# Small matmuls of an attention and routing kernel put on column tiles of TensorE, logits of four batches in one go, counts of a group moved to GpSimd

## The chip, the cores and the metric

The kernel runs on one core of one Trainium2 chip. The metric is the device time of one execution in microseconds (us); lower is better. Three runs of the kernel before gave 476.44, 477.48 and 478.11 us, a median of 477.48.

## The reference, cut to what matters

Two blocks follow each other. The first is a linear attention with a state (four batches, eight heads, 768 steps, head size 48); its output, as 3072 rows of 384, goes through a router with eight experts, of which each row takes one.

```python
# per step t; state is [B, H, 48, 48]
cur = einsum('bhd,bhe->bhde', u * kt, vt)
y[:, :, t] = einsum('bhd,bhde->bhe', rt, state + cur)
state = w * state + einsum('bhd,bhe->bhde', kt, vt)
...
# router: rows x [3072, 384], 8 experts
logits = normed(x) @ normed(expert_emb).T / tau
expert_idx = argmax(logits, axis=1)
gate_w = softmax(logits)[row, expert_idx]
out[mask] = gate_w[mask, None] * (relu(x[mask] @ w1[e]) @ w2[e])    # mask: the rows of expert e
```

Everything is float32 (f32).

## The kernel before, in words

The steps are cut into six chunks of 128. A *unit* is one chunk of one batch, 24 in all, unit i being batch i % 4 of chunk i // 4. The four units of one chunk are a *group*; routing is done by group. `attention` (L713) writes out the order of the work by hand: one loop over i from -1 to 30, in each of whose turns a list of small functions adds instructions for this unit, the next, or one that lies behind. `on` calls a function for one unit, `of_group` for one batch of a group, `whole` once in four turns, when the unit it is given is its group's last. Each engine runs its instructions in the order in which the loop wrote them, and a semaphore makes an engine wait for another.

What a turn i does, in TensorE's order:

- `turn` (L298) transposes the R and the scaled K of unit i+1: `rt` (L304), then `kt` (L309), four matmuls each. VectorE multiplies `rt` by powers of the decay (L306), ScalarE copies `kt` (L311).
- `states` (L330) makes the chunk's K'V for unit i, two heads at a time: four matmuls `st` (L339) with 112 columns of weights and 96 columns streamed, of which the diagonal blocks are used. `carry` (L343) adds them to the state on VectorE (L352), and GpSimd multiplies the state by the decay (L356). The last chunk has no `st`.
- `sums` (L359) makes y of unit i: with the state (L369), and with the masked scores, head by head, on two column halves of the array (L372). ScalarE copies it (L378, L382).
- `scores` (L315) makes the scores of unit i+1, `at` (L322), eight matmuls on two row halves; VectorE masks both tiles (L326).
- `rows` (L387) transposes y into rows, `yrows` (L394); VectorE adds the own term and writes X (L398). `own_sum` follows on VectorE (L286); ScalarE scales by it (`own_rows`, L294, eight instructions).
- `turn_rows` (L471) transposes X of unit i-1, `xp` (L476), and ScalarE copies it to xT (L478).
- `logits` (L486) makes the logits of unit i-2: three matmuls `lg` (L491) with xT as weights (128 columns) and eight streamed columns, the experts.
- In some turns: `ranks` (L510), five matmuls that count, for each row of the group, the rows before it with the same expert (L514 to L517), and `taken` (L578), four matmuls that put the group's row numbers into lists (L581).

The routing of a group on the other engines: `choose` (L494) finds each row's expert on VectorE and leaves a one-hot tile `oh`; `gates` (L520) takes a power on GpSimd (L522), an exponential on ScalarE (L526) and steps on VectorE (L523 to L530); `places` (L533) multiplies rank and one-hot (L536, L538) and adds the group's counts to `cum` on GpSimd, four instructions (L540). `listed` (L574) compares and multiplies (L555 to L570), `summed` (L586) adds the list on VectorE.

PSUM is handed out by tag (`Banks`, L1033): two buffers for "tp", which `rt`, `kt` and `yrows` share in turn, two for "at", and one for each of "st" (`st`, `rank`, `take`, `cp`), "y", "xp" and "lg". A tile waits until the readers of the one that had its buffer before are done.

After turn 24 the loop mixes the routing of the last groups with the first tile of two experts (`Early`, L804): `hidden` (L828, two halves of 12 matmuls), `rows` (L840, two halves of four) and `out` (L849). Then comes the expert stage (`expert`, L903), which fills the rest of the run. `load` (L249) asks for K, R and V of unit i + AHEAD at the start of turn i, on SyncE's queue, where `put` (L543) also writes X out.

Of the kernel before, what the change touches and what calls it, by code (L numbers as in the profile page):

```python
# [19 lines left out]
C = 128  # L20
# [6 lines left out]
TM = 4  # L27
# [12 lines left out]
AHEAD = 5  # L40
# [71 lines left out]
def build_consts(k):  # L112
# [37 lines left out]
    k.qt = numbers(k, "qt", [QS, QS], [[TM, 2], [0, E], [1, TM]], 0, 0)  # L150
    k.turned = numbers(k, "turned", [QS, QS], [[0, 2], [1, E], [0, TM]], 1, 0)
    k.part = pool.tile([QS, 1], I32, name="part")
# [9 lines left out]
    k.sums = pool.tile([QS, 128], F32, name="sums")  # L162
# [5 lines left out]
def build_turned(k):  # L168
# [4 lines left out]
    bits = pool.tile([QS, 3], I32, name="bits")  # L173
    nc.vector.tensor_scalar(bits[:, 0:1], k.part, 2, E - 1, ALU.arith_shift_right, ALU.bitwise_and)
    nc.vector.tensor_scalar(bits[:, 1:2], k.part, 3, None, ALU.bitwise_and)
    nc.vector.tensor_scalar(bits[:, 2:3], k.part, 5, 2, ALU.arith_shift_right, ALU.arith_shift_left)
    own = pool.tile([QS, 3], F32, name="own")
    nc.vector.tensor_copy(own, bits)
    nc.vector.tensor_add(own[:, 1:2], own[:, 1:2], own[:, 2:3])
    k.mask = pool.tile([QS, E], F32, name="mask")  # L180
    nc.vector.tensor_scalar(k.mask, k.number[0:QS], own[:, 0:1], None, ALU.is_equal)
# [26 lines left out]
def build_experts(k):  # L208
# [16 lines left out]
    k.ent = k.const.tile([128, NK, E], F32, name="ent")  # L225
    nc.vector.tensor_copy(k.ent, ps)
# [103 lines left out]
def states(k, i):  # L330

    nc = k.nc
    c, b = divmod(i, B)
    if c == NCH - 1:
        return
    V, Kw = k.loaded[i][2], k.Kpad[i % len(k.Kpad)]
    st = k.ps.tile([128, NP, 2 * D], F32, name="st", tag="st")
    for p in range(NP):
        nc.tensor.matmul(st[0:PP, p, :], pair(Kw, p)[:, 0:PP], pair(V, p), start=True, stop=True)  # L339
    k.st[i] = st  # L340


def carry(k, i):  # L343
# [5 lines left out]
    for s in range(2):  # L349
        rows = slice(s * DP, s * DP + D)  # L350
        part = T[rows, :, s * DP : s * DP + D]
        nc.vector.tensor_add(part, part, st[rows, :, s * D : (s + 1) * D])  # L352
# [118 lines left out]
def turn_rows(k, g, b):  # L471
# [5 lines left out]
    g.xT[b] = k.work.tile([128, NK, C], F32, name="xT", tag="xT")  # L477
# [8 lines left out]
def logits(k, g, b):  # L486
    xT = g.xT.pop(b)
    if b == 0:
        g.lg = k.ps.tile([128, B, E], F32, name="lg", tag="lg")
    for m in range(NK):  # L490
        k.nc.tensor.matmul(g.lg[:, b, :], xT[:, m, :], k.ent[:, m, :], start=(m == 0), stop=(m == NK - 1))  # L491
# [17 lines left out]

def ranks(k, g):  # L510

    mm = k.nc.tensor.matmul
    g.rank = k.ps.tile([128, B, E], F32, name="rank", tag="st")
    mm(g.rank, k.umask, g.oh, start=True, stop=False)  # L514
    for b in range(1, B):
        mm(g.rank[:, b:B, :], k.ones, g.oh[:, 0 : B - b, :], start=False, stop=False, skip_group_check=True)
    mm(g.rank, k.ones, k.cum[:, None, :].to_broadcast([128, B, E]), start=False, stop=True)  # L517
# [15 lines left out]
def places(k, g):  # L533
# [5 lines left out]
    for b in range(B):  # L539
        nc.gpsimd.tensor_add(k.cum, k.cum, g.oh[:, b, :])  # L540
# [37 lines left out]
def taken(k, g):  # L578
    g.take = k.ps.tile([QS, 128], F32, name="take", tag="st")
    for b in range(B):  # L580
        k.nc.tensor.matmul(  # L581
            g.take, g.what[:, b].rearrange("p q s -> p (q s)"), g.lane[:, b, :], start=(b == 0), stop=(b == B - 1)
        )
# [73 lines left out]
def turner(k, by):  # L657

    nc, p = k.nc, k.rt
    hit = p.tile([QS, E], F32, name="hit", tag="hit")  # L660
    rank = p.tile([QS, 1], F32, name="myrank", tag="myrank")
    nc.vector.scalar_tensor_tensor(hit, by[0:QS], 1.0, k.mask, ALU.mult, ALU.mult, accum_out=rank)
    perm = p.tile([QS, QS], F32, name="perm", tag="perm")
# [39 lines left out]
def route(k, g):  # L703
    for b in range(B):
# [3 lines left out]
        logits(k, g, b)  # L708
    for step in (choose, ranks, gates, places):
# [3 lines left out]
def attention(k):  # L713
# [17 lines left out]
    for i in range(-1, units + 7):  # L731
# [6 lines left out]
        whole(places, i - 4)  # L738
        on(own_rows, i)
        on(turn, i + 1)  # L740
        on(scaled, i + 2)
# [3 lines left out]
        whole(choose, i - 3)  # L745
        whole(listed, i - 5)
# [11 lines left out]
        of_group(logits, i - 2)  # L758
# [376 lines left out]
```

## Time and profile before

| | |
|---|---|
| runs before, us | 476.44, 477.48, 478.11 (median 477.48) |
| profiled execution, us | 475.24 |
| its span, first to last instruction, us | 473.4 |
| granted TensorE clock over the span | 0.99 |
| busy: TensorE, its weight loads | 447.4 us (95%), 317.5 us (67%) |
| busy: VectorE, ScalarE, GpSimd | 148.8 us (31%), 138.2 us (29%), 171.7 us (36%) |
| moved by DMA | 54.26 MB, mean 115 GB/s |
| 40 to 150 us | the attention's units, one after another |
| 178 to 205 us | routing of the last groups and the two early tiles |
| 205 us to the end | the experts |

All lines of the profile are of one profiled execution of 475.24 us, of which 473.4 lie between its first and last instruction. PE is TensorE's matmuls, PEld its weight loads, DVE is VectorE, ACT is ScalarE, POOL is GpSimd, SP is SyncE, which issues DMAs; L322 is line 322 of the kernel. In a timeline the first number is the start in us from the span's start, the second how long the instruction or the row of like instructions took; x8 is their number, and a bracket tells how long the engine was idle before it and what ended that. Each f32 matmul of the program is recorded as two MATMULs, with a weight load each (transposes as one). The ends of matmuls are modelled and overlap, so the distance between starts is the better measure of what one costs.

### The profile page before, as it was taken

What the parts mean: (1) busy time and instruction counts of PE and PEld (TensorE: products, weight loads), DVE (VectorE), ACT (ScalarE), POOL (GpSimd) and SP (SyncE); (2) the same over time, 40 slices, a digit from 0 to 9 for tenths busy, and PEclk for the clock granted to TensorE, in tenths of its full rate; (3) what the DMA queues carried; (4) which work ended last, traced back from release to release, by engine and by line L of the source; (5) the groups of instructions that cost most, each with busy time, mean ns of one, the idle gap of its engine ahead of it and who ended that gap; (6) DMA issues with size and microseconds to landing.
All of it is one profiled execution on the core that took longest, in us unless ns stands there. A gap on an engine that the chain in (4) does not pass through costs nothing.

```text
span 473.4 us, 7292 instructions
## 1 busy us (share of the span) xinstructions
PE 447.4 (95%) x2716; PEld 317.5 (67%) x2716; DVE 148.8 (31%) x416; ACT 138.2 (29%) x410; POOL 171.7 (36%) x260
## 2 busy tenths in 40 slices
PE   8789999999999889999999999999998999999990
PEld 3578889898989778866765555555555555556550
DVE  4556776566657754230102003003002002011010
ACT  2376655665565561101101201201210200201200
POOL 7766677665856433360204003303301201011010
PEclk9999999999999999999999999999999999999996
DMA  8766645654561393143535125134232243100000
GB/s 177 141 135 136 134 95 108 135 127 106 105 135 35 106 406 123 47 138 133 184 150 200 27 106 198 57 133 149 103 133 87 113 151 120 46 18 32 1 37 19
DMA packets 93791, 54.26 MB, mean 115 GB/s; under 512 B 76937, under 2 KB 88380, under 8 KB 93746
## 3 DMA queue, kind: packets, MB, share of 16 engines
q1 hardware_dynamic: 89024, 43.85, 33.6%
q0 software_dynamic: 3296, 9.44, 5.6%
q10 hardware_dynamic: 1426, 0.41, 0.4%
q8 instruction: 23, 0.38, 0.3%
q14 instruction: 22, 0.18, 0.1%
HBM read 44.45 MB, written 9.63 MB: 114 GB/s over the span
## 4 chain that ended last, share of the span: by engine, by line
PE 79%; DVE 9%; ACT 4%; SPq 2%; issue 2%; DMA 2%; POOL 1%; POOLq 0%; ACTq 0%; DVEq 0%
PE ps L920 26%; PE ps L938 14%; PE ps L928 11%; PE at L322 5%; PE y L372 3%; PE y L369 3%; PE st L339 3%; PE early_h L834 2%; DVE AT L326 2%; ACT xd L294 2%; PE lg L491 2%; PE early_y L845 2%; PE yrows L394 2%; DVE y L940 1%; PE kt L309 1%
## 5 line engine op out<-in xcount | busy, mean ns | idle before, releaser
L920 PE MATMUL ps<-xTe,w 128*128 128x384 f32 (+3 forms) x384 | 120.9, 475 | 3.0 <-DVE xTe L915 2.8
L920 PEld LDWEIGHTS ps<-xTe,w 128*128 128x128 f32 x384 | 72.3, 190 | 48.3 <-issue 22.3
L941 POOL DMA_INDIRECT out_dram<-y,to x25 | 24.7, 987 | 205.0 <-DVE y L940 186.7
L940 DVE TENSOR_SCALAR y<-ps,gates 128x384 f32<-128x384 f32 (+2 forms) x25 | 14.6, 613 | 229.4 <-PE ps L938 125.2
L921 ACT ACTIVATE hT<-ps 128x384 f32<-128x384 f32 (+3 forms) x64 | 30.2, 478 | 165.3 <-PE ps L920 165.2
L938 PE MATMUL ps<-w,hT 128*128 128x384 f32 x208 | 67.9, 486 | 0.0
L938 PEld LDWEIGHTS ps<-w,hT 128*128 128x128 f32 x208 | 39.5, 190 | 27.1
L928 PE MATMUL ps<-hT,w 128*128 128x416 f32 (+1 forms) x144 | 52.0, 521 | 0.0
L294 ACT ACTIVATE xd<-V,diag 128x48 f32<-128x48 f32 x192 | 45.8, 321 | 19.3 <-DVE diag L286 14.9
L928 PEld LDWEIGHTS ps<-hT,w 128*128 128x128 f32 x144 | 27.4, 190 | 24.2 <-issue 24.2
L326 DVE TENSOR_TENSOR AT<-at,umask 128x512 f32<-128x512 f32 x48 | 30.9, 686 | 34.2 <-PE at L322 34.2
L322 PE MATMUL at<-RT,KT 48*128 48x128 f32 x384 | 27.9, 285 | 4.4 <-ACT KT L311 3.4
L356 POOL TENSOR_TENSOR state<-state,wpow 48x192 f32<-48x192 f32 x40 | 20.4, 511 | 28.0 <-DVE state L352 26.5
L887 POOL DMA_INDIRECT G<-xs,take x25 | 25.2, 1008 | 12.2 <-issue 5.8
L322 PEld LDWEIGHTS at<-RT,KT 48*128 48x128 f32 x384 | 23.3, 187 | 9.3 <-ACT KT L311 5.1
L372 PE MATMUL y<-AT,V 128*48 128x128 f32 x384 | 25.9, 277 | 0.0
L280 POOL TENSOR_TENSOR KU<-KU,Rpad 128x384 f32<-128x384 f32 x24 | 24.1, 1003 | 1.9
L271 POOL TENSOR_TENSOR Kpad<-K,kpow 128x384 f32<-128x384 f32 x23 | 23.1, 1003 | 3.3 <-DVE kpow L100 2.0
L279 POOL TENSOR_TENSOR KU<-K,u_bc 128x384 f32<-128x384 f32 x24 | 24.1, 1003 | 0.3 <-DVE diag L286 0.3
L372 PEld LDWEIGHTS y<-AT,V 128*48 128x48 f32 x384 | 19.8, 122 | 3.0
L369 PE MATMUL y<-RT,state 128*112 128x128 f32 x160 | 21.2, 275 | 0.0
L478 ACT COPY xT<-xp 128x384 f32<-128x384 f32 x24 | 11.5, 480 | 31.3 <-PE xp L476 31.3
(183 smaller groups left out, 515.1 us busy)
## 6 DMA issues: line engine op xcount, KB each, us to landing
w<-in_moe_w_dram SPq DMA_DIRECT2D x16, 1536.0 KB, 6.3
K<-in_k_dram SPq DMA_DIRECT2D x24, 192.0 KB, 3.6
V<-in_v_dram SPq DMA_DIRECT2D x24, 192.0 KB, 3.5
xs<-X SPq DMA_DIRECT2D x24, 192.0 KB, 2.0
Rpad<-in_r_dram SPq DMA_DIRECT2D x23, 192.0 KB, 3.6
G<-xs,take POOLq DMA_INDIRECT x27
out_dram<-y,to POOLq DMA_INDIRECT x25
Rpad<-in_r_dram ACTq DMA_DIRECT2D x1, 192.0 KB, 4.0
```

The lines of the kernel that those rows point to most:

```text
L279: nc.gpsimd.tensor_mul(KU, K, k.u_bc)
L294: k.nc.scalar.mul(xd[:, h, :], V[:, h, :], diag[:, h : h + 1])
L322: nc.tensor.matmul(at[s][:, p, :], KT[rows, p, :], RT[rows, p, :], start=True, stop=True)
L326: nc.vector.tensor_mul(a, at[s], k.umask[:, None, :].to_broadcast([128, NP, C]))
L369: mm(y[0:PP, p, :], T[:, p, 0:PP], RT[:, p, :], start=(p == 0), stop=False, skip_group_check=True)
L372: mm(y[s * DP : s * DP + D, p, :], V[:, 2 * p + s, :], AT[s][:, p, :], start=(c == 0 and p == 0), stop=True, skip_group_check=True,)
L887: nc.gpsimd.indirect_dma_start(out=G[0:n, :], out_offset=None, in_=k.xs[:, :], in_offset=IndirectOffsetOnAxis(ap=take[0:n], axis=0), bound ...
L920: mm(ps[:, 0:n], w1[:, m, f * 128 : (f + 1) * 128], xT[:, m, 0:n], start=(m == 0), stop=(m == NK - 1))
L921: nc.scalar.activation(hT[:, f, 0:n], ps[:, 0:n], ACT.Relu)
L928: mm(ps[:, 0:n], w2[:, f, m * 128 : (m + 1) * 128], hT[:, f, 0:n], start=(f == 0), stop=(f == NF - 1))
L938: mm(ps, hT[:, f, at], w2[:, f, :], start=(f == 0), stop=(f == NF - 1))
L941: nc.gpsimd.indirect_dma_start(out=k.out[:, :], out_offset=IndirectOffsetOnAxis(ap=to[0:here], axis=0), in_=y[0:here, :], in_offset=None, ...
```

## The change

Five things, of which four lie on TensorE.

- `states`: one matmul for each head in place of one for two heads, 48 columns of weights and 48 streamed; even heads write rows 0 to 47, odd heads rows 64 to 111, so the two lie on different column halves. `carry` reads the smaller tile.
- `logits`: runs once for a group, with the expert embeddings as weights (32 columns, of which eight are used) and xT streamed (128 columns); batch b goes to column quarter b, four batches side by side. The result has experts on partitions; `logits_out` copies it to SBUF on ScalarE, and `turn_logits` transposes it on TensorE. The tile `lgT` uses the tag "st". xT gets five buffers.
- `ranks`: GpSimd makes the counts ahead of each batch (`before`, one copy and four additions, the last of which updates `cum`), and two matmuls replace five. The additions in `places` go.
- `taken`: batches 0 and 2 sum on one column half, 1 and 3 on the other; the tiles of the lists (`sums`, `qt`, `turned`, `mask`, `hit`, `perm`) have 128 rows in place of 64.
- AHEAD is 4 in place of 5, which gives back the memory of one unit's K, R and V.

```diff
-AHEAD = 5
+AHEAD = 4
...
-    k.ent = k.const.tile([128, NK, E], F32, name="ent")
-    nc.vector.tensor_copy(k.ent, ps)
+    k.ent = k.const.tile([128, NK, 32], F32, name="ent")
+    nc.vector.memset(k.ent, 0.0)
+    nc.vector.tensor_copy(k.ent[:, :, 0:E], ps)
...
 def states(k, i):
-    st = k.ps.tile([128, NP, 2 * D], F32, name="st", tag="st")
+    st = k.ps.tile([128, NP, D], F32, name="st", tag="st")
     for p in range(NP):
-        nc.tensor.matmul(st[0:PP, p, :], pair(Kw, p)[:, 0:PP], pair(V, p), start=True, stop=True)
+        for s in range(2):
+            h = 2 * p + s
+            nc.tensor.matmul(
+                st[s * DP : s * DP + D, p, :], Kw[:, h, 0:D], V[:, h, :], start=True, stop=True, skip_group_check=True
+            )
...
-        nc.vector.tensor_add(part, part, st[rows, :, s * D : (s + 1) * D])
+        nc.vector.tensor_add(part, part, st[rows])
...
-def logits(k, g, b):
-    xT = g.xT.pop(b)
-    if b == 0:
-        g.lg = k.ps.tile([128, B, E], F32, name="lg", tag="lg")
+def logits(k, g):
+    mm = k.nc.tensor.matmul
+    lgT = k.ps.tile([128, 128], F32, name="lgT", tag="st")
     for m in range(NK):
-        k.nc.tensor.matmul(g.lg[:, b, :], xT[:, m, :], k.ent[:, m, :], start=(m == 0), stop=(m == NK - 1))
+        for b in range(B):
+            mm(
+                lgT[b * 32 : (b + 1) * 32, :], k.ent[:, m, :], g.xT[b][:, m, :],
+                start=(m == 0), stop=(m == NK - 1), tile_position=(0, b * 32), skip_group_check=True,
+            )
+    g.lgT = lgT
+def logits_out(k, g):
+    t = k.rt.tile([128, 128], F32, name="lgT", tag="lgT")
+    k.nc.scalar.copy(t, g.lgT)
+    g.lgT = t
+def turn_logits(k, g):
+    lg = k.ps.tile([128, B, 32], F32, name="lg", tag="lg")
+    k.nc.tensor.transpose(lg.rearrange("q b e -> q (b e)"), g.lgT, k.ident)
+    g.lg = lg[:, :, 0:E]
...
+def before(k, g):
+    nc = k.nc
+    g.pre = k.rt.tile([128, B, E], F32, name="pre", tag="pre")
+    nc.gpsimd.tensor_copy(g.pre[:, 0, :], k.cum)
+    for b in range(1, B):
+        nc.gpsimd.tensor_add(g.pre[:, b, :], g.pre[:, b - 1, :], g.oh[:, b - 1, :])
+    nc.gpsimd.tensor_add(k.cum, g.pre[:, B - 1, :], g.oh[:, B - 1, :])
 def ranks(k, g):
     mm(g.rank, k.umask, g.oh, start=True, stop=False)
-    for b in range(1, B):
-        mm(g.rank[:, b:B, :], k.ones, g.oh[:, 0 : B - b, :], start=False, stop=False, skip_group_check=True)
-    mm(g.rank, k.ones, k.cum[:, None, :].to_broadcast([128, B, E]), start=False, stop=True)
+    mm(g.rank, k.ones, g.pre, start=False, stop=True)
...
 def places(k, g):
-    for b in range(B):
-        nc.gpsimd.tensor_add(k.cum, k.cum, g.oh[:, b, :])
...
 def taken(k, g):
-    g.take = k.ps.tile([QS, 128], F32, name="take", tag="st")
+    g.take = k.ps.tile([2 * QS, 128], F32, name="take", tag="st")
     for b in range(B):
         k.nc.tensor.matmul(
-            g.take, g.what[:, b].rearrange("p q s -> p (q s)"), g.lane[:, b, :], start=(b == 0), stop=(b == B - 1)
+            g.take[b % 2 * QS : (b % 2 + 1) * QS], g.what[:, b].rearrange("p q s -> p (q s)"), g.lane[:, b, :],
+            start=(b < 2), stop=(b >= B - 2), skip_group_check=True,
         )
...
 def attention(k):
         whole(places, i - 4)
+        whole(logits_out, i - 3)
         on(own_rows, i)
         on(turn, i + 1)
+        whole(turn_logits, i - 3)
         on(scaled, i + 2)
         on(own, i + 1)
         on(states, i)
         of_group(squares, i - 1)
         whole(choose, i - 3)
+        whole(before, i - 3)
         whole(listed, i - 5)
...
         of_group(turn_rows, i - 1)
-        of_group(logits, i - 2)
+        whole(logits, i - 2)
         whole(ranks, i - 3)
         whole(gates, i - 3)
```

## The prediction

> **What bounds the kernel now.** First the page's slices: from 40 us on TensorE is at 9 to 10 tenths in nearly every slice, and the chain that ended last is TensorE's.
>
> ```profile
> PE   8789999999999889999999999999998999999990
> PE 79%; DVE 9%; ACT 4%; SPq 2%; issue 2%; DMA 2%; POOL 1%; POOLq 0%; ACTq 0%; DVEq 0%
> ```
>
> Busy isn't bound, so next the timeline of one plain unit of the attention:
>
> ```profile
> 94.18 0.60 PE L394 MATMUL yrows<-ident,yT 112*128 112x112 f32 x4
> 94.28 1.29 DVE L326 TENSOR_TENSOR AT<-at,umask 128x512 f32<-128x512 f32 x2 [1.36 <-PE at L322]
> 94.62 0.49 PE L476 MATMUL xp<-ident,X 128*128 128x128 f32 x3
> 94.95 0.73 PE L491 MATMUL lg<-ent,xT 128*128 128x8 f32 x6
> 95.49 0.55 DVE L398 TENSOR_TENSOR X<-yrows,xd 128x384 f32<-128x384 f32 x1
> 95.54 0.64 PE L304 MATMUL rt<-ident,Rpad 128*128 128x128 f32 x4
> 96.18 0.63 PE L309 MATMUL kt<-ident,Kpad 128*128 128x128 f32 x4
> ```
>
> The "tp" buffers hand yrows' place to kt, so kt waits for X, and X waits behind the two maskings on DVE. X ends at 96.04; kt starts 0.14 later. In the other plain units it is the same. So kt starts 2.0 us after yrows whatever TensorE does between; it has 0.1 to 0.2 to spare there already. Counting from yrows to yrows, a group takes 6.32 (plain), 7.24 (with take), 6.32 (its choose) and 7.80 (with ranks): 27.68 us, four times over. In the last of these another DVE chain ends late:
>
> ```profile
> 145.39 0.16 DVE L536 TENSOR_TENSOR at<-rank,oh 128x32 f32<-128x32 f32 x1
> 145.60 0.53 PE L339 MATMUL st<-V,Kpad 128*112 128x96 f32 x3 [0.32 <-DVE at L536]
> ```
>
> st waits for places to read rank (they share a bank), and places stands behind X, diag and the gates, not behind TensorE's ranks. Last the tail, where TensorE is full and each routing step hides beside an early tile:
>
> ```profile
> 182.71 2.92 PE L834 MATMUL early_h<-earlyx,w 128*128 128x128 f32 x24
> 182.90 0.19 DVE L498 TENSOR_REDUCE mx<-lg 128x4 f32<-128x32 f32 x1 [0.49 <-PE lg L491]
> 183.79 0.19 DVE L504 TENSOR_TENSOR oh<-oh,first 128x32 f32<-128x32 f32 x1
> 185.47 0.31 PE L514 MATMUL rank<-oh,umask 128*128 128x32 f32 x2
> 185.67 0.60 ACT L838 ACTIVATE earlyh<-early_h 128x512 f32<-128x512 f32 x1 [3.96 <-PE early_h L834]
> 186.51 2.83 PE L845 MATMUL early_y<-w,earlyh 128*128 128x384 f32 x8
> 188.98 0.40 POOL L570 TENSOR_TENSOR what<-sel,gate 128x128 f32<-128x128 f32 x1
> 189.44 1.09 PE L581 MATMUL take<-lane,what 128*64 128x128 f32 x8
> ```
>
> The choice of experts (182.9 to 184.0) lies wholly under early_h.
>
> [...] y's matmuls on two halves (L372) start in pairs 7 ns apart, a pair every 109 ns, and wherever the mode changes 203 ns pass in place of 109: a drain of 94. The first weight load is then exposed too. [...] with few columns streamed, 128 of weights give 111 ns a MATMUL (L491), 112 give 98 (L339), and L372's loads of 48 follow 42 apart. [...]
>
> **Part by part.** The sum is made against the profiled 475.24 us (span 473.4); the median 477.48 lies 2.24 above, and the difference is carried over.
>
> *st, 20 units, 16 of them (4 to 19) in the steady stage; in the first four, ACT's chain (diag, eight xd, KT) sets the pace.* Before: 8 x 98 = 785 ns. After: 16 MATMULs in 8 pairs. A pair costs the larger of 48 streamed columns (48/128 of 109 = 41) and the load (42), say 45: 360. The mode changes add 94+42 going in and 94+93 (y's 112 columns) coming out: 683. Gain 0.10. After ranks the drain hides in the wait, and the exposed load shrinks from 76 to 42: 861 to 589, gain 0.27. No row streams pairs this fast: L372 sustains 27 ns per MATMUL or load, and at that pace a pair is 109 and st 1195, a loss of 0.41; bounds -0.1 to +0.41. I take 45, since at 84.27 to 84.32, where L372 begins, four loads and two MATMULs start within 48 ns.
>
> *logits.* Removed from plain units: 6 x 111 = 0.67 each, worth nothing, since kt waits for X. In one turn of four: 24 MATMULs, four at a time, 6 x 109 = 654, entry 94+28, exit 94+59: 0.93. xp and yrows 0.77, rt 0.44, so kt at 2.14 instead of 2.0: +0.14, and the transpose +0.11. Two at a time (the only packing in the trace) would make it 0.65 more; less than 6 rounds can't be. logits_out queues on ACT ahead of xd, but ends (about 2.05) before diag frees xd (2.4), and before kt ends, so the transpose finds it ready.
>
> *ranks.* 10 MATMULs of 112 become 4, 0.67 less, worth nothing: X and then places set the end. `before` (five ops of about 0.23 to 0.26) moves past the state's multiply and the power on POOL: the power ends at 142.4, DVE asks at 143.97; one op more fits. *take.* 8 x 109 to 4 x 109: kt would be free at 1.94, so X binds and the unit falls from 7.24 to 6.32: -0.92. Bounds 0 (no pairing) to -0.92.
>
> *AHEAD, ent, the 128-row lists.* Nothing: K lands 3.6 us after its issue and is asked for units later. Load 5 now stands behind put 0 on SP: issue 23.8, landing 27.5, asked by POOL's L271 at 32.6. Without that cover POOL stalls by the excess.
>
> Steady stage: five plain units x -0.10, three with take x -1.02, four after ranks x -0.27, four with lgT x +0.15 (0.14+0.11-0.10): -4.0.
>
> *Tail.* In turn 22 `before` stands on POOL ahead of the two early gathers, whose end the power, exp, xd and yT wait for: +0.38. No lg before early_x: -0.57. lgT uses "st", so it waits for summed after take: take 0.53, wait 0.55, lgT 0.75, then early_h's drain and exposed load 0.20, against 1.71: +0.32. Then what costs: in the changed program's order logits_out stands on ACT behind both earlyh activations, and on PE the transpose stands behind early_h, ranks behind it, early_y behind ranks. So the choice no longer lies under early_h but after it. With T the end of early_h (185.47 before): earlyh (0.60) ends T+0.8, logits_out (about 0.30: L108's copy of 128x128 took 297 ns) T+1.1, the transpose reaches DVE at T+1.5 (0.3 from a matmul's start to DVE's, as for mx), choose's five steps (1.08, from 182.90 to 183.98) T+2.6, three additions on POOL (0.26 each, L540's four took 1.04) T+3.45, ranks end T+3.8. early_y waited until T+1.0 before: stall 2.8. The power (L522, 1.02), which ran at 180.0, long before it was asked for, now stands behind `before` on POOL and ends at T+4.75; gates' steps, exp and places (2.05, put together from 184.00 to 184.60 and 186.17 to 187.33 and the hand-overs) T+6.8, lists (1.2, L555 to L565) T+8.0, what (0.8) T+8.85. take finds TensorE idle since T+6.4: stall 2.5. The second half of early_y starts at T+9.6, before at 190.45 = T+5.0: +4.6. Bounds: +2.3 if half of these latencies overlap, +6 if the idle array loses clock; across a gap of 1.8 us at 173 the granted clock stayed 1.00. The experts behind are unchanged. Tail: +4.7.
>
> Sum: -4.0 + 4.7 = +0.7: profiled 475.9, median 478.2. This case's own range is 476.4 to 480.0, from 1.8 less to 1.8 more: a pair at 45 to 55 in st, and half a microsecond either way for each of the two stalls.
>
> **Rivals.** *Slower: st's pairs are bound by issue.* One mechanism, 16 units; it decides from 58 ns a pair ((785-323)/8). At 90, st is 1043, 0.36 more than I took: 16 x 0.36 = 5.8, time 484.0. For it: sustained pace in L372. Against: the burst at 84.28. *lgT two at a time:* 0.65 x 5 = 3.3 (four units and the tail), time 481.5. For it: two is all that the trace shows. [...] *Faster: X isn't what holds kt.* Then each of 12 steady units drops 0.6 more: -7, time 471. Against: kt follows X by 0.1 in unit after unit. *Tail overlaps more,* +2.3 instead of +4.6: 475.9. For it: ACT and DVE often start before the row ahead has ended. Against: the steps feed each other, one result at a time. That the change doesn't do what it says is excluded for order: the built program has it as told.
>
> **Chances.** Forecast 0.50, issue-bound 0.22, two at a time 0.12, kt free 0.08, tail hidden 0.08. A difference below 0.3% (1.4 us) can't be told from none here. Of the forecast 0.03 is faster, 0.36 same, 0.11 slower; of the tail case half faster. Faster 0.15, same 0.40, slower 0.45. Range 475.2 to 484.2: it leaves out about 0.1 at each end.
>
> **What would show it.** Right: plain units near 6.2 with kt still 0.1 behind X; take units down to plain; st still waiting for places; two idle stretches of 2 to 3 us on TensorE after the second early_h. Wrong: st over 0.8 us, lgT over 1.2 us, units below 6.0, or POOL or DMA ahead of kt.

## The result, and the profile after

The changed kernel takes 489.01 us (median; 488.34 to 492.32), the kernel before 477.46 beside it (476.44 to 478.11): 1.0258 times as long, 95% interval 1.0207 to 1.0309. The forecast was 478.2, with a range that ended at 484.2. The profiled execution took 488.37 us, its span is 486.5 (before 475.24 and 473.4). So 13.1 us were lost in the profile, where +0.7 was forecast. Executions of one kernel fall into groups here: of the kernel before, 23 of them beside one set of experiments, ten took 475.1 to 475.8 us at a granted clock of 0.990 to 0.994 and thirteen 477.3 to 478.3 at 0.986 or 0.987, so a median moves by up to 2 us with their mix, and small differences are judged by the interval.

The page's slices of the kernel after, first TensorE's busy tenths, then the granted clock in tenths, then the engines' shares of the chain that ended last; below them the clock's slices of the kernel before:

```profile
PE   8778979797997869799999999999999999999990
PEclk9999999899998997899999999999999999999996
PE 79%; DVE 12%; ACT 4%; issue 2%; POOL 1%; POOLq 0%; DVEq 0%; ACTq 0%
```

```profile
PEclk9999999999999999999999999999999999999996
```

In the kernel before every slice of the clock but the last is a 9, and VectorE (DVE) has 9% of the chain. Now four slices, the 8th, 13th, 16th and 17th, are lower, and VectorE has 12%. A stretch with a granted clock of 0.5 is called *half clock* from here on. Where the time went is read from one landmark, the start of yrows in each unit, in both traces. Measured from the first unit in which a state is carried (46.05 before, 46.04 after):

| stretch | before, us | after, us | difference | forecast |
|---|---|---|---|---|
| each plain unit | 6.32 | 6.21 | -0.11 | -0.10 |
| each unit with take | 7.24 | 6.21 | -1.03 | -1.02 |
| each unit with the logits | 6.32 | 6.44 | +0.12 | +0.15 |
| the four units after ranks | 7.80 each | 8.33, 10.59, 10.09, 10.23 | +8.0 in all | -1.1 in all |
| steady stage in all, to yrows of unit 19 | 103.5 | 108.5 | +5.0 | -4.0 |
| from there to the end | 323.8 | 331.9 | +8.1 | +4.7 |

Three of the four kinds of unit are as forecast. The timeline of a unit with take, in the kernel after, answers to the plain unit shown of before:

```profile
73.24 0.60 PE L399 MATMUL yrows<-ident,yT 112*128 112x112 f32 x4
73.68 0.49 PE L481 MATMUL xp<-ident,X 128*128 128x128 f32 x3
74.11 0.66 PE L609 MATMUL take<-lane,what 128*64 128x128 f32 x8
74.55 0.55 DVE L403 TENSOR_TENSOR X<-yrows,xd 128x384 f32<-128x384 f32 x1
74.70 0.66 PE L305 MATMUL rt<-ident,Rpad 128*128 128x128 f32 x4
75.19 0.62 PE L310 MATMUL kt<-ident,Kpad 128*128 128x128 f32 x4
```

X ends at 75.10 and kt starts 0.09 later, 1.95 after yrows: the wait that bound the plain unit before binds this one too, and take's 0.92 is gone.

The unit after ranks is where the forecast broke. The kernel after, the second such unit, with GpSimd (POOL) beside VectorE:

```profile
87.14 1.00 POOL L272 TENSOR_TENSOR Kpad<-K,kpow 128x384 f32<-128x384 f32 x1
87.21 0.55 DVE L403 TENSOR_TENSOR X<-yrows,xd 128x384 f32<-128x384 f32 x1
88.10 1.00 POOL L280 TENSOR_TENSOR KU<-K,u_bc 128x384 f32<-128x384 f32 x1
88.14 0.98 DVE L553 TENSOR_SCALAR ssq<-ssq 128x4 f32<-128x4 f32 x1
89.17 0.99 POOL L281 TENSOR_TENSOR KU<-KU,Rpad 128x384 f32<-128x384 f32 x1
89.37 0.85 DVE L555 TENSOR_TENSOR l<-l,ssq 128x32 f32<-128x32 f32 x1
91.03 0.16 DVE L566 TENSOR_TENSOR at<-rank,oh 128x32 f32<-128x32 f32 x1
91.24 0.56 PE L342 MATMUL st<-V,Kpad 128*48 128x48 f32 x16 [2.77 <-DVE at L566]
...
92.79 1.88 PE L377 MATMUL y<-AT,V 128*48 128x128 f32 x16
94.60 1.97 PE L323 MATMUL at<-RT,KT 48*128 48x128 f32 x16
```

Two things are to be seen. First, a step of VectorE on four numbers a row takes 0.98 us, and it ends at 89.12, 0.02 after the product of GpSimd that it overlaps; another takes 0.85 and ends 0.06 after the next product. The same two lines in the kernel before, while GpSimd waited for ranks, and GpSimd's lines there:

```profile
88.61 0.16 DVE L523 TENSOR_SCALAR ssq<-ssq 128x4 f32<-128x4 f32 x1
...
89.01 0.19 DVE L525 TENSOR_TENSOR l<-l,ssq 128x32 f32<-128x32 f32 x1
89.10 1.04 POOL L540 TENSOR_TENSOR cum<-cum,oh 128x8 f32<-128x8 f32 x4 [1.74 <-PE rank L517]
...
90.10 1.00 POOL L271 TENSOR_TENSOR Kpad<-K,kpow 128x384 f32<-128x384 f32 x1
```

Here the additions to cum wait 1.74 us for ranks on TensorE, and everything behind them on GpSimd's queue (Kpad, KU) waits too: Kpad starts at 90.10, when the gates are nearly done. The change moved the additions into `before`, and Kpad and KU came forward onto the gates. X (87.21 after), with one operand in PSUM and one in SBUF, runs under Kpad at its usual 0.55. Second, y and at take 1.88 and 1.97 where they take 1.08 and 1.16 elsewhere: from 92.9 to 96.3 the granted clock is 0.5, right behind the idle 2.77 us of TensorE. That happens after three of the four waits (2.77, 2.42 and 2.41 us); behind the first, of 2.11, the clock stays at 1.0.

The tail behaves as forecast in kind. The kernel after, the second half of the first early_h having ended at about 194.7:

```profile
194.85 0.60 ACT L869 ACTIVATE earlyh<-early_h 128x512 f32<-128x512 f32 x1 [4.12 <-PE early_h L865]
195.35 0.26 ACT L506 COPY lgT<-lgT 128x128 f32<-128x128 f32 x1
195.66 0.33 PE L512 MATMUL lg<-ident,lgT 128*128 128x128 f32 x1 [0.84 <-ACT lgT L506]
...
198.07 0.41 PE L547 MATMUL rank<-pre,ones 128*128 128x32 f32 x2 [0.43 <-POOL pre L538]
...
198.31 4.52 PE L876 MATMUL early_y<-w,earlyh 128*128 128x384 f32 x8
...
203.26 0.66 PE L609 MATMUL take<-lane,what 128*64 128x128 f32 x8 [0.43 <-POOL what L598]
```

The logits' copy stands behind earlyh, and the choice no longer lies under early_h. What stands ahead in an engine's queue holds up what is ready behind it: the last MATMULs of lgT start at 191.67, the copy of it at 195.35, behind earlyh, although ScalarE idled 4.12 us ahead of earlyh. early_y starts about 3.6 us after early_h's end and then, at half clock, takes 4.52 in place of 2.83. The second stall that was forecast, 2.5 us ahead of take, shows as 0.43 only, since the slow early_y fills the rest of it.

### The profile page after: what moved, and what is told of

Same layout as the page of the kernel before. It is cut to its first block, busy times and chain, and to the rows that moved or that the text cites. A ratio compares the mean times of both kernels' runs of the same rounds, so it can differ in the third digit from the quotient of the medians.

```text
span 486.5 us, 7552 instructions
## 1 busy us (share of the span) xinstructions
PE 439.8 (90%) x2846; PEld 301.0 (62%) x2846; DVE 155.3 (32%) x417; ACT 139.7 (29%) x416; POOL 171.4 (35%) x265
## 4 chain that ended last, share of the span: by engine, by line
PE 79%; DVE 12%; ACT 4%; issue 2%; POOL 1%; POOLq 0%; DVEq 0%; ACTq 0%
PE ps L951 25%; PE ps L969 14%; PE ps L959 11%; PE at L323 5%; PE y L377 4%; PE y L374 4%; DVE AT L327 3%; PE early_h L865 2%; PE wake L66 2%; ACT xd L295 2%; PE st L342 2%; PE early_y L876 2%; DVE y L971 1%; PE yrows L399 1%; PE kt L310 1%
## 5 line engine op out<-in xcount | busy, mean ns | idle before, releaser
L323 PE MATMUL at<-RT,KT 48*128 48x128 f32 x384 | 29.5, 296 | 7.2 <-ACT KT L312 5.4
L323 PEld LDWEIGHTS at<-RT,KT 48*128 48x128 f32 x384 | 24.9, 198 | 12.4 <-ACT KT L312 6.9
L377 PE MATMUL y<-AT,V 128*48 128x128 f32 x384 | 27.8, 290 | 0.0
L374 PE MATMUL y<-RT,state 128*112 128x128 f32 x160 | 23.2, 290 | 0.0
L377 PEld LDWEIGHTS y<-AT,V 128*48 128x48 f32 x384 | 21.5, 129 | 2.8 <-issue 0.2
```

The lines of the kernel that those rows point to most:

```text
L323: nc.tensor.matmul(at[s][:, p, :], KT[rows, p, :], RT[rows, p, :], start=True, stop=True)
L374: mm(y[0:PP, p, :], T[:, p, 0:PP], RT[:, p, :], start=(p == 0), stop=False, skip_group_check=True)
L377: mm(y[s * DP : s * DP + D, p, :], V[:, 2 * p + s, :], AT[s][:, p, :], start=(c == 0 and p == 0), stop=True, skip_group_check=True,)
```

## The experiments

Theory 1: VectorE's gate steps stand still while GpSimd multiplies (the collision), TensorE idles longer ahead of st, and after idling so long it has half clock for 3.41 us, the length of one such stretch in the traces (a *window*). Theory 2: the clock falls because the change took work off TensorE, wherever. Theory 3, beside either: the tail's loss is the order of the logits' steps. The kernel before ran beside each set; the table gives its median there, and the ratio on record with its 95% interval (it is not the quotient of the two medians).

| kernel | what it is | median, us | before beside it | ratio | interval |
|---|---|---|---|---|---|
| e1_hold | changed kernel, GpSimd held until the gates are done | 480.25 | 475.33 | 1.0116 | 1.0094 to 1.0138 |
| e2_warm | changed, five unread products in the wait | 490.00 | 475.33 | 1.0312 | 1.0295 to 1.0329 |
| e3_counts_only | before, with the counts alone | 492.29 | 475.33 | 1.0344 | 1.0322 to 1.0366 |
| e5_counts_back | changed, counts as they were | 477.77 | 475.33 | 1.0065 | 1.0013 to 1.0117 |
| e2b_warm3 | changed, three unread products in the wait | 483.93 | 476.49 | 1.0124 | 1.0085 to 1.0164 |
| e4_tail | e1_hold, and the tail reordered | 476.20 | 476.49 | 0.9980 | 0.9959 to 1.0001 |
| e6_gathers | e1_hold, and the early gathers later | 478.34 | 476.49 | 1.0033 | 1.0008 to 1.0059 |
| e7_both | e1_hold, tail and gathers | 475.52 | 476.49 | 0.9960 | 0.9935 to 0.9986 |
| e8_warm_gaps | e7_both, idle stretches filled | 473.93 | 475.86 | 0.9946 | 0.9926 to 0.9966 |
| s_st | before, with the state's update packed | 472.27 | 475.86 | 0.9917 | 0.9892 to 0.9941 |
| s_take | before, with the slices packed | 472.74 | 475.86 | 0.9917 | 0.9888 to 0.9946 |
| s_logits | before, with the logits packed | 484.71 | 475.86 | 1.0167 | 1.0120 to 1.0213 |
| c_counts_held | e3_counts_only, GpSimd held | 482.40 | 477.49 | 1.0108 | 1.0069 to 1.0147 |
| c_logits_held | s_logits, GpSimd held, tail reordered | 476.00 | 477.49 | 0.9976 | 0.9961 to 0.9991 |
| c_st_take | before, with state and slices packed | 471.35 | 477.49 | 0.9889 | 0.9842 to 0.9936 |
| c_warm_gaps2 | e8_warm_gaps, one filling moved | 470.77 | 477.49 | 0.9875 | 0.9838 to 0.9913 |

### GpSimd held until the gates are done

```diff
 def places(k, g):
...
         nc.vector.reduce_sum(k.pos[:, g.c, :], at, axis=AX.X)
+    held = p.tile([128, B], F32, name="held", tag="held")
+    nc.gpsimd.tensor_copy(held, k.gate[:, g.c, :])
```

> The changed kernel, with one small copy on GpSimd in places that reads the finished gates, so that Kpad and KU no longer run over the gates' steps on VectorE. Theory 1 (VectorE's small steps of the gates stand still while GpSimd multiplies, and the idle TensorE then loses its clock): the add to ssq falls from 0.98 back to about 0.16 us, l from 0.85 to about 0.19, the four units after ranks from 8.33, 10.59, 10.09 and 10.23 to about 7.5 each, no half clock before 160 us, time about 480. Theory 2 (the clock falls because the change took work off TensorE, whatever GpSimd does): the units lose only the 0.8 us of the collision, the half-clock windows at 93, 120 and 151 us stay, time about 486. If GpSimd's later start holds up Kpad or diag instead: units of 8 us or more with a wait for L272 or L281.

The timeline of the same unit in this kernel:

```profile
86.59 0.16 DVE L553 TENSOR_SCALAR ssq<-ssq 128x4 f32<-128x4 f32 x1
...
87.00 0.19 DVE L555 TENSOR_TENSOR l<-l,ssq 128x32 f32<-128x32 f32 x1
...
88.15 0.19 POOL L570 COPY held<-gate 128x4 f32<-128x4 f32 x1 [2.51 <-DVE gate L560]
88.22 0.56 PE L342 MATMUL st<-V,Kpad 128*48 128x48 f32 x16 [1.29 <-DVE at L566]
```

One more instruction on GpSimd, and both steps are back at 0.16 and 0.19. The four units after ranks take 7.51, 7.51, 7.51 and 7.52 us, where the prediction had worked out 7.53; the clock stays at 1.0 until 170 us. From yrows of unit 4 to that of unit 19 the kernel is 4.2 us shorter than the kernel before, where the prediction had -4.0. Kpad starts 3.9 us after yrows, 2.7 later than in the changed kernel, and no unit grows by it. Theory 1 as expected; theory 2 falls for these units, as far as it said that the lighter units lose the clock whatever GpSimd does. The trace is of an execution of 476.92 us, the median is 480.25; what the longer executions lose, and whether it is half clock behind the waits of 1.29, no trace shows.

### The counts alone, and all but the counts

To the kernel before only `before` and the short `ranks` were added, and the additions in `places` taken out, in diff form:

```diff
+def before(k, g):
...
+    nc.gpsimd.tensor_copy(g.pre[:, 0, :], k.cum)
...
 def places(k, g):
...
-    for b in range(B):
-        nc.gpsimd.tensor_add(k.cum, k.cum, g.oh[:, b, :])
```

> The kernel before, with only the counts of the group on GpSimd (before, and ranks of four MATMULs); state, logits and slices as they were. Theory 1: with the additions gone from places nothing holds Kpad and KU back, so they run over the gates: the add to ssq takes about 1 us, the units after ranks rise from 7.80 to 8.4 or more, time 480, and 486 if the clock falls too. Theory 2: the removed MATMULs were not on the path and the clock falls only with all the packing: 477.5, no half clock.

The kernel with the counts alone, its second unit after ranks:

```profile
91.75 0.99 DVE L531 TENSOR_SCALAR ssq<-ssq 128x4 f32<-128x4 f32 x1
...
92.99 0.85 DVE L533 TENSOR_TENSOR l<-l,ssq 128x32 f32<-128x32 f32 x1
...
94.87 1.23 PE L339 MATMUL st<-V,Kpad 128*112 128x96 f32 x8 [2.47 <-DVE at L544]
```

The same collision without any packing, and half clock behind all four waits: 10.9 us in two of these units and 10.5 in the other two, where 7.80 stood. That is 12 of the 17 us lost; the rest comes at the end of the routing, where the clock is halved too (188 to 198 us). It is more than the 486 expected: a unit at half clock had been put 1 us too short, and the end was left out. The other way round, the changed kernel with ranks and the additions as they were:

```diff
 def places(k, g):
...
+    for b in range(B):
+        nc.gpsimd.tensor_add(k.cum, k.cum, g.oh[:, b, :])
...
-        whole(before, i - 3)
```

> The changed kernel with ranks and the additions to cum as they were before the change (counts of the group on TensorE, additions in places); state, logits and slices packed. Theory 1: units after ranks 7.5 to 7.8 us, no half clock before 160 us, time about 480, the rest being the tail. Theory 2 (packing alone takes too much work off TensorE): half clock stays in some of these units, time 484 to 488.

477.77: most of the loss is gone. The units after ranks take 8.06 us, more than the 7.5 to 7.8 expected: with the logits' matmuls gone from the unit, ranks come earlier, the additions too, and Kpad reaches one step of the gates (the addition of 1e-9, 0.69 us in place of 0.17). So the collision doesn't belong to the counts as such; it belongs to when Kpad is let go.

### The clock by itself

Unread products put into the wait, the collision left as it is:

```diff
+def warm(k, g):
+    if g.c < NCH - 2:
+        ps = k.ps.tile([128, 512], F32, name="warm", tag="xp")
+        for _ in range(5):
+            k.nc.tensor.matmul(ps, k.ones, k.rpow.rearrange("q p c -> q (p c)"), start=True, stop=True)
...
+        whole(warm, i - 4)
```

> The changed kernel, with five extra products of 128x512 on TensorE between kt and st in the four units after ranks (about 2.3 us; their result isn't read). The collision stays. If the clock is what makes three of these units 2 us longer than the first: the granted clock stays 1.0 up to 160 us, all four units near 8.3 us, time about 483, although TensorE does more. If the collision alone makes them so long: 10.1 to 10.6 stay, time 489. If the added work itself is on the path: all units above 8.5, time above 489.

The five products were mis-sized: each is two instructions of 0.45 us, 4.46 in all, and they held st up:

```profile
89.40 4.46 PE L745 MATMUL warm<-rpow,ones 128*128 128x512 f32 x10
...
93.79 0.56 PE L342 MATMUL st<-V,Kpad 128*48 128x48 f32 x16
```

All four units take 10.45, and the time is 490.0. Nothing follows for the clock's part but that it stayed at 1.0 in these units. With `range(3)` in place of `range(5)`:

> The changed kernel with three extra products of 128x512 after kt in the four units after ranks (six instructions of 0.45 us, 2.7 us, in a gap of 2.8; five took 4.46 us and held st up by 1.5). Collision theory with the clock as its second part: no half clock before 160 us, the four units 8.3 to 8.5 us each, 5 us less by unit 20, time 484. If the clock has no part in the length of these units: 10.1 to 10.6 us, time 489.

```profile
90.10 2.74 PE L745 MATMUL warm<-rpow,ones 128*128 128x512 f32 x6
93.06 0.56 PE L342 MATMUL st<-V,Kpad 128*48 128x48 f32 x16 [0.22 <-DVE at L566]
```

The units take 8.73, 9.01, 8.73 and 8.73 us at full clock, 35.2 in all where the changed kernel needs 39.2, and the time is 483.9: TensorE does more and the kernel is faster. That is a little more than the 8.3 to 8.5 expected: in three units st now starts right behind the products, and in the second, shown, the collision is longer than in the first. With the collision in place, then, the clock is what makes units of over 10 us. The split is read from the idle stretch ahead of st. In e1_hold it is 1.29 us, in the changed kernel 2.11, 2.77, 2.42 and 2.41: the collision's own part is the difference, 4.5 in the four units. Together they are 9.2 us longer than in e1_hold, so 4.7 are the clock's, 1.5 to 1.6 for each of the three windows. The 9.01 above agrees: 7.51 and the 1.48 by which the second stretch is longer.

### The tail, and unit 22

On the kernel with GpSimd held, the last group's copy, transpose, choice and `before` go ahead of the second half of the first early_h:

```diff
         if i == units + 1:
+            for f in (logits_out, turn_logits, choose, before):
+                f(k, k.groups[NCH - 1])
             first[0].hidden(1)
```

(and their places in unit 26 are left empty.)

> The kernel with GpSimd held (480.25 us), and in addition the last group's copy of the logits, transpose, choice and before put ahead of the second half of the first early_h in every queue. Tail theory (these steps stood behind earlyh and early_h): the choice lies under early_h, early_y starts within 0.7 us of its end (before 3.5), take waits at most 1 us after the first half of early_y, early_y at full clock; the second half of early_y 3 us earlier, time 477. Rival (the tail is bound by the chain before early_h, or by take to lists behind it): less than 1 us, time 479.5 to 480.

```profile
181.11 2.84 PE L872 MATMUL early_h<-earlyx,w 128*128 128x128 f32 x24
...
184.15 2.83 PE L883 MATMUL early_y<-w,earlyh 128*128 128x384 f32 x8
...
188.57 0.66 PE L611 MATMUL take<-lane,what 128*64 128x128 f32 x8 [1.59 <-POOL what L600]
```

early_y follows early_h by 0.2 us at full clock; the second half of early_y starts 3.3 us earlier (189.15 for 192.45). take still waits 1.59, more than the 1 expected: the lists start only after ranks, which stand behind early_h. The ratio falls from 1.0116 to 0.9980. Theory 3 holds for this part.

In unit 22 the two early gathers follow `before` on GpSimd, and the power that exp, xd and yT wait for follows the gathers. They are put behind the power:

```diff
-            first = [Early(k, r, *lists, w) for r, w in zip(LAST, k.weights)]
...
         whole(gates, i - 3)
+        if j == 10:
+            first = [Early(k, r, *lists, w) for r, w in zip(LAST, k.weights)]
```

> The kernel with GpSimd held (480.25 us), and in addition the two early gathers put behind the power of gates on GpSimd's queue. Theory (before pushes the gathers and the power back, exp and xd wait for the power, the idle TensorE then loses half its clock for two windows): yrows' wait of 4.19 us falls to 2 or less, 1.5 us earlier, and if no window is lost then 1 to 3 us more: time 476 to 478.7. Rival (gathers later make early_x late): early_x waits for its rows, time 480 or more.

> Held GpSimd, tail order and gathers behind the power together. If the two gains add: 5 to 7 us under 480.25, 473 to 475, level with the kernel before or a little faster. If one only moves the stall to the other's place: no better than the better of the two.

yrows of unit 23 waits 2.67 us in place of 4.19 (2 or less was expected), because exp, and xd behind it on ACT, now wait for VectorE's gate steps, which stand behind diag. By the ratio it is worth 0.8%; together with the tail's order the ratio is 0.9960, little under the 0.9980 of the tail's order alone, whose interval it overlaps. By the ratios the gains don't add, and 473 to 475 is just missed. In the profile of the two together the half clock came at 89 and 144 us as well, behind waits of 1.29 us, which e1_hold and e4_tail had without it; that execution took 477.6 us, where the median is 475.52. So how much of the two gains adds is open.

### Idle stretches filled

On the last kernel, unread products in the idle stretches that are left (`warm(k, 1)` ahead of st after ranks, `warm(k, 2)` behind carry of units 20 and 23):

> The kernel with held GpSimd, tail order and gathers behind the power (475.5 us; half clock in windows at 161 and 174 to 178 us, in some profiles at 89 and 143 too), and in addition unread products of 128x512 in its idle stretches: one after kt in the four units after ranks (0.89 us in a gap of 1.3), two after y in unit 20 (1.78 in 1.8, while VectorE settles) and two after y in unit 23 (1.78 in 2.7). If the clock falls because these stretches leave a window half idle: no half clock between 40 and 180 us, 3 to 5 us less, 470.5 to 472.5. If the clock isn't what these stretches cost: 475.5 or more.

Right for unit 23 (yrows waits 0.75, early_h takes 2.84 and not 4.16), wrong for unit 20: the stretch in which VectorE settles lies one unit later. There the products made unit 20 longer by 1.5 us, and the half clock at 158 to 165 stayed. 473.9. Moved by one unit:

> The run with filled gaps again, with the two products of unit 20 moved one unit on, to where TensorE idles 1.8 us while VectorE settles (in unit 20 they lengthened the unit by 1.5 and left that gap as it was, with the half clock behind it). If the half clock follows from the idle stretch: no half clock between 40 and 180 us, unit 21 near 7.4 us in place of 8.2, 471. If it doesn't: half clock at 155 to 165 us again, 473 or more.

The clock's slices of this kernel, from its page, and unit 21:

```profile
PEclk9999999999999999999999999999999999999996
```

```profile
154.77 1.99 PE L746 MATMUL warm<-rpow,ones 128*128 128x512 f32 x4
156.78 1.16 PE L323 MATMUL at<-RT,KT 48*128 48x128 f32 x16
157.87 0.60 PE L399 MATMUL yrows<-ident,yT 112*128 112x112 f32 x4
```

No half clock is left but at the very end, where the kernel before has it too; unit 21 takes 7.48, and the time is 470.8, as expected. The whole change is in this kernel; with its four remedies (GpSimd held, the tail's order, the gathers' place, filled stretches) it takes 0.9875 of the kernel before.

### One part at a time

Each of the first three is the kernel before with the hunks of one part of the diff.

> The kernel before, with only the state's update packed (16 MATMULs on two column tiles). As forecast step by step: 0.10 us less in twelve units, 0.27 in the four after ranks, 2.3 us in all, 474.2 where the kernel before has 476.5. Issue-bound rival: 3 us more. If freed time only idles: 476.5.

> The kernel before, with only the slices packed (take on two halves, lists with 128 rows). As forecast: 0.92 us less in three units and 0.5 less in two places of the tail, 3 to 4 us in all, 473 where the kernel before has 476.5. Rival: unit 20's chain on VectorE and the tail give it back, 475 to 476.5.

> The kernel before, with only the logits packed (four batches in one go, copy and transpose, loads one unit less ahead). As forecast: 0.25 us more in four units, 4.6 to 4.9 more in the tail, 482 where the kernel before has 476.5; the half clock beside early_y would make it 484. Rival (the tail's stall comes from the counts, not from the logits' order): 477 to 478.

State alone: plain units 6.22 and units after ranks 7.52, so 0.10 and 0.28 less where 0.10 and 0.27 were forecast. Its span is 3.3 shorter, but 0.7 of that lies ahead of the first yrows, a stretch that takes 20.8 to 22.6 us over these profiles, whatever part is in; from there on it is 2.6 shorter. Slices alone: 6.81 for the unit with take in place of 7.24, so 0.43 and not 0.92, because with the logits' matmuls still in that unit TensorE sets kt's start (X ends at 74.79, kt starts at 75.44, right behind rt); from the first yrows on 2.6 less. Logits alone lose 1.7%: the unit with the logits takes 6.54 (forecast 6.57), but the units after ranks take 9.90, 8.37, 9.97 and 8.37, by a collision (a gate step of 0.17 takes 0.69) and half clock in two of them, and in the tail early_y takes 5.47.

> The kernel before with only the logits packed (484.7), and both remedies: GpSimd held until the gates are done, and in the tail the copy, transpose and choice ahead of the second half of the first early_h. If the packed logits lose only by the same two mechanisms: units after ranks near 7.8 (before 9.9, 8.4, 10.0 and 8.4), early_y within 0.7 us of early_h, 476 to 478. If packing the logits costs elsewhere: 480 or more.

With both remedies the units after ranks are at 7.81, early_y starts 0.9 us behind early_h (0.7 was expected), and the logits alone stand at 0.9976: what they lost was the collision, the clock behind it and the tail's order, and little else. AHEAD of 4 is in this run too, so it costs little at most; alone it was not run.

> The kernel before with only the counts of the group on GpSimd, as in the run that took 492.3, and GpSimd held until the gates are done. If the collision of Kpad and KU with the gates is the whole reason for that run's 16 us (3 us in each of four units after ranks, the rest behind the lost clock): units after ranks 7.5 to 7.8, no half clock before 180 us, 476 to 478. If the counts cost something in another place (the additions themselves, the later power, the tail): 480 or more.

Here it falls that the collision is the whole reason: the units after ranks are at 7.81 and keep their clock, yet the kernel is at 1.0108. The timeline of units 22 and 23:

```profile
168.69 1.30 POOL L822 DMA_INDIRECT G<-xs,take  x1 [0.75 <-issue]
...
171.33 1.04 POOL L530 TENSOR_TENSOR ssq<-ssq,half 128x4 f32<-128x4 f32 x1
...
176.11 0.60 PE L394 MATMUL yrows<-ident,yT 112*128 112x112 f32 x4 [3.45 <-ACT yT L378]
...
181.10 5.47 PE L843 MATMUL early_h<-earlyx,w 128*128 128x128 f32 x24
```

The power starts 2.59 us after yrows of unit 22 (before: 1.36), yrows waits 3.45 (before 1.55), and then the clock is halved for three windows, early_h taking 5.47 in place of 2.92. So the counts cost a second time, where `before` stands ahead of the gathers and the power: the first gather starts 1.5 us after the list it reads was written, 0.75 of them behind the end of `before`, where it started 0.3 after its list in the kernel before.

> The kernel before with state and slices packed, logits and counts as they were. If the gains add (3.9 us each alone): 468 where the kernel before has 476. If the stretch in which VectorE settles takes the second one back, by its wait or by a half clock behind it: 470 to 472.

The two gaining parts without the others: 0.9889, 471.4, level with the whole change and its remedies. Counted from the first yrows the profile is 4.8 us shorter, alone 2.6 each, so in the profiles the gains nearly add. (The 3.9 each of the expectation came from the ratios of times, not from the traces.) TensorE waits 1.27 us in unit 21 while VectorE settles (before 0.84), without a half clock. Both parts take work off TensorE, and it keeps its clock: theory 2 fails here as well.

## Why the prediction was wrong

**The step that failed** is the one on ranks: "`before` (five ops of about 0.23 to 0.26) moves past the state's multiply and the power on POOL: the power ends at 142.4, DVE asks at 143.97; one op more fits", together with "0.67 less, worth nothing: X and then places set the end". It asked what the moved steps delay on GpSimd. It didn't ask what is let go where they were taken from: the additions had held Kpad and KU back, GpSimd idling 1.74 us for ranks ahead of them, and Kpad and KU without them run where the gates run. What was put at nothing came to 9.2 us in four units. The forecast for these units was right for the kernel in which the additions' wait is put back in another form (7.51 against 7.53). The trace shows the collision: both steps start after the product beside them and end 0.02 and 0.06 us behind it. In the four units the addition to ssq starts 0.02, 0.04, 0.38 and 0.39 us after a product and takes 0.16, 0.98, 0.64 and 0.63; the last three end within 0.03 us of the product's end, the first keeps its time. The reciprocal behind it keeps 0.18 beside these products, and X, with one input in PSUM, its 0.55. That the steps wait for GpSimd's product is shown by e1_hold, where they take 0.16 and 0.19 without it; what inside the chip makes them wait, no run shows. The kernel before showed it already: settled (L630) took 0.69 and is_e (L650) 0.97 beside KU. No rival named it.

**The clock** was a bound of the tail alone ("+6 if the idle array loses clock; across a gap of 1.8 us at 173 the granted clock stayed 1.00"). One gap that wasn't followed by half clock was taken as a rule, and in the steady stage the term was put at nothing. By the profiles here, one execution of each kernel, over the four waits of st after ranks:

| idle of TensorE ahead of st, us | kernels | half clock behind it |
|---|---|---|
| 0.3 | before, s_st, c_st_take | 0 of 12 |
| 0.98 | c_counts_held, c_logits_held | 0 of 8 |
| 1.29 | e1_hold, e4_tail, e6_gathers, e7_both | 3 of 16 |
| 1.53 | e5_counts_back, s_logits | 2 of 8 |
| 2.1 to 2.8 | the changed kernel, e3_counts_only | 7 of 8 |

Behind these waits it lasts 3.41 us each time, and it followed waits from 1.29 to 2.77 us.

Why the same wait is followed by half clock in one execution and not in another, the traces show in large part. In each of the 13 that have more than one half-clock stretch, these begin a whole number of 3.413 us apart, to 0.001 us, the one at the very end included; in the changed kernel the others begin 8, 17, 22, 26, 31 and 113 times that behind the first. So the clock of these executions goes by windows of 3.413 us on a grid, which lies differently in each of them, and by the counts below it goes with how much of TensorE's idle time falls into one window. In the changed kernel, two windows around the first wait and two around the second (from:to, length, TensorE busy and its instructions, clock, then DMA's share and GB/s):

```profile
58.78:62.19 3.41, 2.34 (x19) 1.00 0.46 110
62.19:65.60 3.41, 2.23 (x36) 1.00 0.89 171
89.50:92.91 3.41, 1.67 (x26) 1.00 0.87 169
92.91:96.32 3.41, 3.41 (x32) 0.50 0.00 0
```

An edge cut the first wait, and its 2.11 us cost no clock; most of the second lay in one window, 1.74 us idle, and the next had half clock. In the profiles of the kernel before and of the changed kernel, in windows at full clock from 40 to 205 us, none of 82 with less than 1.3 us idle was followed by half clock, and all of six with 1.75 to 3.02 were. Over all 18 profiles: of 769 with less than 1.3 us idle none was followed by half clock, of 21 with 1.3 to 1.7 five were, of 31 with more all were. Of the sixteen waits of 1.29, an edge cut eight, and none of these had half clock behind it; of the eight that lay whole in one window three had. What parts those three from the other five is open. The gap at 173 that the prediction leaned on, 1.55 us by the matmuls' records, was cut by an edge into 0.39 and 1.16: that it kept its clock was luck of that execution.

**The sum.** Forecast -4.0 in the steady stage, measured +5.0. The 9.0 between them are the collision (4.5) and the clock behind it (4.7), 9.2 together, by the units of e1_hold and of the changed kernel. In the tail forecast +4.7, measured +8.1. The stall ahead of early_y came to 2.6 (forecast 2.8), the second half of early_y at 9.2 us after early_h's end (forecast 9.6): right in kind and order, and in size for the sum, though half clock stands where the second idle stretch was forecast. Mis-sized was unit 22, "+0.38" for `before` ahead of the gathers: from yrows of unit 22 to that of unit 23 it was 1.25, and c_counts_held shows the same 1.23 at full clock. Left out was the clock: 1.32 from yrows of unit 21 to that of unit 22, behind an idle stretch of 1.80 us in unit 21 (before 0.84), and about 1.9 from yrows of unit 23 to the end of early_h, whose first half takes 3.97 in place of 2.92. The stretch in unit 21 is one that the packed kernels have and the kernel before has not, with the unit as long as before: work taken off TensorE there only idles, and then costs clock. In this one place theory 2 holds.

**What was right.** kt waits for X in plain units; a pair in st at 45 ns (the pairs start 45 ns apart in the trace after, behind a first one of 80; 16 MATMULs take 0.56 us, so the issue-bound rival, 90 ns a pair, is out); the changes of tile form around st (in the trace after, st starts 202 ns behind the transpose ahead of it, where 109 pass between transposes, and y 144 behind the last pair, where 45 pass between pairs, its second MATMUL 201 behind its first, where 109 pass later: with the first pair's 80 that is about 320 ns over the plain pace, forecast 323; "drain" is the author's word for part of it, and what the array does in that time no trace shows); lgT four at a time, the four starting 5 to 8 ns apart and a round every 109 ns behind a first of 133, 0.86 us at full clock (so not two at a time, though two was all that the trace of before had shown, and four an estimate of the author's); take's unit down to a plain one; ranks' fewer MATMULs worth nothing (c_counts_held: 7.81 with them gone). In the parts alone the 0.92 of take was 0.43: the prediction's figure needed the logits' matmuls gone as well, which it didn't say.

## What to carry to other kernels

Before an instruction is taken from an engine's queue, look at what waits behind it there: a wait that costs nothing by itself can be what keeps two engines apart, and its removal brings the rest of the queue forward onto another engine's steps. On a chain of small VectorE steps that TensorE waits for, look at what GpSimd runs beside them, and compare each step's time there with its time elsewhere: here a TENSOR_SCALAR went from 0.16 to 0.98 us and a TENSOR_TENSOR with both operands in SBUF from 0.19 to 0.85, while a reciprocal kept 0.18 and a step with one operand in PSUM 0.55. Price an idle stretch of TensorE with the half clock that may follow it (here stretches from 1.29 us on, and 1.5 to 1.6 us each time behind ranks), do not take one that kept its clock for a rule, and test it by putting unread products into it: if the granted clock stays up and more work makes the kernel faster, it was the clock.

## What was unexpected of the hardware

- A VectorE step of 0.16 us took 0.98 beside a GpSimd product of 1.00, and ended with it; the product stayed at 1.00.
- Idle stretches of 1.29 to 2.77 us ahead of st, none of which filled a window, were followed 12 times of 32 by half clock for one window of 3.41 us, in the tail for up to three; over 1.7 us idle in one window of the grid was followed by it 31 times of 31, less than 1.3 never in 769; 2.7 us of unread products in the stretch kept it at 1.0 and made the kernel 1.3% faster (1.0124 against 1.0258, each beside its own runs of the kernel before).
- Sixteen MATMULs of 48 columns on two column tiles took 0.56 us, a pair every 45 ns, with 7 ns between the two of a pair.
